# Planner limits, ScalarE squares and DMA moves in a fused attention, mixture-of-experts and MLP kernel

## The chip, the cores and the metric

The kernel runs on 1 core of one Trainium2 chip. The metric is the device time of one execution in microseconds (us), the median of the runs shown.

## The reference

Attention over pooled keys and values gives 4608 tokens of 512 numbers. A router assigns each token to one of 8 experts, in the order of the logits, with 576 places for each expert. Each expert is a two-layer network with a relu, and a shared two-layer network with a squared relu follows.

```python
def _moe_ref(x, w_gate, w1, w2):
    logits = x @ w_gate
    order = np.argsort(-logits.flatten())
    ...
    for idx in order:
        tok, e = int(idx) // E, int(idx) % E
        if assigned[tok] >= 0 or counts[e] >= cap:
            continue
        assigned[tok] = e
        counts[e] += 1
    ...
    for e in range(E):
        mask = assigned == e
        h = np.maximum(x[mask] @ w1[e], 0.0)
        out[mask] = h @ w2[e]

def _moe2_ref(x, w_in, w_out):
    r = np.maximum(x @ w_in, 0.0)
    return (r * r) @ w_out
```

The sizes are: attention 8 batches of 8 heads, 576 positions, 64 wide; experts 512 to 1024 to 512; the shared network 512 to 2048 to 512. All of it is float32.

## The kernel before

The work has three parts. First comes attention, which writes the tokens to DRAM. Then the experts follow one after the other; each expert's 576 tokens run through four products on TensorE (PE). Beside these, from the first expert on, the routing of the later experts runs in the background.

**One expert** is `mlp(n)`, n from 0 to 7. Layer 1 (512 to 1024) and layer 2 (1024 to 512) use the function `layer`, whose matmuls stand at L1249. Layer 3 (512 to 2048) is followed by relu and square, and the last product (2048 to 512, matmuls at L1441 in `last_layer`) is scaled and scattered to the output. A float32 number is carried as two float16 halves, high and low, so each product is three passes (`PASSES`), and each result is split again: ScalarE (ACT) writes the high half, and GpSimd (POOL) or VectorE (DVE) subtracts it to get the low half.

**Layer 3 of expert 0** also goes through `layer` (L1249), with 16 output tiles, each of 576 columns. `plain3` empties a tile: ACT scales it into a float32 work tile (`copy`, L1402), DVE does relu and square in one instruction (`square`, L1411), and `parts1` writes the high half on ACT (L1487) and the low half on POOL (L1488). There are three PSUM buffers for the tiles (`mmt`).

**Layer 3 of experts 1 to 7** needs fewer products, by mixed weights and mixed inputs (seven products instead of eight for each of four output groups, L1386, in the order `ORDER`). It is emptied by `copy` and `relu` on ACT, `join` (L1406) and `square` (L1411) on DVE, and `parts` on ACT and POOL (L1417, L1418). The mixed weights are made by `mix_first` during expert 0 and the start of expert 1: 16 pieces, loaded by SP, combined on POOL, split on ACT and POOL, stored by SP. It sets the event "mixed" when it is done and the loads of the first six have been queued; layer 3 of expert 1 waits for that.

**The background.** The order of all instructions is set while the program is built, by a small planner, the class `Background`. Each engine executes its own instructions in that order. The planner keeps an account in microseconds for PE, ACT, DVE and POOL (`pe`, `a`, `v`, `p`); `work` adds an estimated cost to them. `tick` advances PE's account and goes through the tasks. A task is a generator; it runs on to its next `yield` if the time that it last yielded has come and if the accounts of the engines that it uses are no further ahead of PE's than an allowed depth (2.0 us in most places; for DVE also `vdepth`, 0.9 during layer 3 of experts 1 to 7). A `hold` letter keeps tasks that use that engine from running: the products of layer 3 hold back all that use ACT, except in two places per output group (`slot`). Transfers have no account, except for a fixed delay in the gathers.

The tasks that matter here are these:

- `route(n)` finds the tokens of the expert of number n. It has eight iterations for a threshold, each with two matmul steps on PE (L870 and L884) between DVE steps (L849 is the comparison before L870; L873, L877 and L879 lead to L884). It then makes the indices (`idx`, L999). After a DVE step it yields until DVE's account plus 0.35 us, plus `lazy`, which is 0 for the first two routes and 0.8 for the others. Its uses are "rv"; "r" is a mark with no account.
- `fetch(n)` loads the weights of expert n (SP), finds their scale (L1073) and splits them (L1086 on ACT, L1087 on DVE).
- `gather(n)` fetches the tokens with five indirect transfers on POOL (L1150), converts five pieces (L1188 on ACT, L1189 on DVE, into the tile `gfm`, which has two buffers), and transposes each by a DMA from SP (L1190). For n = 1 a piece is due 12 us (`FLIGHT`) after its gather in POOL's account.
- `split_fixed` splits the shared network's second weight into halves, in place, in eight pieces. Four of them come after layer 2 of expert 0: ACT writes the high half into a `gfm` buffer (L760), DVE the low half into another (L762), and DVE copies both into the place of the weight (L763, L764). The last product of expert 0 waits for all eight.

`wait_next` holds the next expert until its weights and tokens have been planned. `last_layer` of one expert therefore runs beside `fetch` and `gather` of the next.

Of the kernel before, what the change touches and what calls it, by code (L numbers as in the profile page):

```python
# [27 lines left out]
NM = CAP // 128  # L28
# [29 lines left out]
class Background:  # L58
# [6 lines left out]
    def __init__(self):  # L65
        self.pe = self.a = self.v = self.p = 0.0
        self.tasks = []
        self.depth = DEPTH
        self.vdepth = 9.9

    def add(self, gen, uses="av"):
        self.tasks.append([0.0, gen, uses, uses])
# [12 lines left out]
    def tick(self, pe=0.0, hold=""):  # L85

        self.pe += pe
        for t in list(self.tasks):
            while (t[0] <= self.pe and not any(e in t[3] for e in hold)
                   and all(getattr(self, e) <= self.pe + (min(self.depth, self.vdepth) if e == "v" else self.depth)  # L90
                           for e in t[3] if e != "r")):
                try:
                    y = next(t[1]) or 0.0
                except StopIteration:
                    self.tasks.remove(t)
                    break
                t[0], t[3] = y if isinstance(y, tuple) else (y, t[2])
# [8 lines left out]
def moe_kernel(  # L106
# [150 lines left out]
    def later():  # L257
        return bg.pe + 0.1
# [492 lines left out]
    def split_fixed():  # L751
# [3 lines left out]
        for c in range(8):  # L755
            f = words(1, c)
            t = wo[:, c].rearrange("p a b f -> p a (b f)")
            if ("l2", 0) in done:
                hi = r_p.tile([128, 512], F32, name="gfm").bitcast(F16)
                A.activation(hi, f, AF.Copy, scale=K["sout"])  # L760
                lo = r_p.tile([128, 512], F32, name="gfm").bitcast(F16)
                V.scalar_tensor_tensor(lo, f, K["sout"], hi, op0=OP.mult, op1=OP.subtract)  # L762
                V.tensor_copy(t[:, 0], hi)  # L763
                V.tensor_copy(t[:, 1], lo)  # L764
                bg.work(a=1.0, v=1.8)
                yield bg.pe + PACE
                continue
            fs = []
# [29 lines left out]
    def route(n):  # L798

        last = n == E - 1  # L800
        lazy = 0.0 if n < 2 else 0.8
        m, mx = m0, first0
        if n:
            m = r_p.tile([128, NI], F32, name="rm")
# [326 lines left out]
    def gather(n):  # L1131
# [24 lines left out]
        if n == 0:  # L1156
# [14 lines left out]
                bg.work(pe=0.45, a=0.6, v=0.7)  # L1171
                yield 0
            return
        if n == 1:
            while ("l3", 0) not in done:
                yield later()
        for _ in range(NM + 1):
            get()
        if n > 1:
            while ("l3", n - 1) not in done:  # L1180
                yield later()
            at = [max(at[c], bg.pe + 4.0 * c) for c in range(NM + 1)]
        xt[n] = r_p.tile([128, 2, HP, CAP], F16, name="xy", bufs=1)
        for c in range(NM + 1):
            yield at[c]
# [89 lines left out]
    def mlp(n, arrive=None):  # L1275
# [121 lines left out]
        def relu(q, p):  # L1397
            A.activation(q, p, AF.Relu, scale=sg["r"])  # L1398
            bg.work(a=0.7)

        def copy(q, p):
            A.activation(q, p, AF.Copy, scale=sg["r"])  # L1402
            bg.work(a=0.7)

        def join(q, p):
            V.scalar_tensor_tensor(q, p, sg["r"], q, op0=OP.mult, op1=OP.add)  # L1406
            bg.work(v=0.75)

        def square(q):

            V.scalar_tensor_tensor(q, q, 0.0, q, op0=OP.max, op1=OP.mult)  # L1411
            bg.work(v=0.8)

        def parts(q, m, half):

# [54 lines left out]
        if n == 0:  # L1470
# [3 lines left out]
            def plain3(m, p):  # L1474
                if m == 0:
                    first3.append(p)
                    return
                for mz, pz in ([(0, first3[0])] if m == 1 else []) + [(m, p)]:
                    q = qs[3 + mz % 3]
                    copy(q, pz)  # L1480
                    square(q)
                    if mz:
                        parts1(mz - 1)

# [15 lines left out]

        wait("mixed")
        b, a, e = mm(), mm(), mm()
        bg.vdepth = 0.9
        tile[0] = a, b, e
        for j, (gr, i) in enumerate(ORDER):
            if i == 1 and gr:
# [54 lines left out]
                square(c12[gr])  # L1561
                parts(c21[gr], 2 * gr + 8, 0)
            bg.tick(hold="a")
        bg.vdepth = 9.9
        parts(c12[3], 6, 1)
        done.add(("l3", n))
        for _ in last:
# [129 lines left out]
```

## Time and profile before

| | us |
|---|---|
| median of 3 runs | 1422.22 |
| lowest and highest | 1414.69 and 1423.02 |
| the profiled execution | 1418.14 |
| its span in the profile | 1416.4 |

The span runs from the first to the last instruction; 1.7 us lie around it. In the profile PE's matmuls and weight loads (PEld) are shown apart. Where an idle time has a releaser, it is the instruction whose end let the waiting one begin. Stages of the profiled execution were set by their matmuls: expert 0 has layer 3 from 286.4 us and its last product from 348.6 to 404.3 us; layer 3 of experts 1, 2 and 3 begins at 454.3, 606.0 and 756.1 us, and that of expert 6 at 1183.4 us; the last product of expert 2 begins at 651.1 us, layer 1 of expert 3 at 702.2 us, the last product of expert 6 at 1221.9 us. Odd experts have a fifth piece in their last product, which takes the places left over from two experts.

### The profile page before, as it was taken

What the parts mean: (1) busy time and instruction counts of PE and PEld (TensorE: products, weight loads), DVE (VectorE), ACT (ScalarE), POOL (GpSimd) and SP (SyncE); (2) the same over time, 40 slices, a digit from 0 to 9 for tenths busy, and PEclk for the clock granted to TensorE, in tenths of its full rate; (3) what the DMA queues carried; (4) which work ended last, traced back from release to release, by engine and by line L of the source; (5) the groups of instructions that cost most, each with busy time, mean ns of one, the idle gap of its engine ahead of it and who ended that gap; (6) DMA issues with size and microseconds to landing.
All of it is one profiled execution on the core that took longest, in us unless ns stands there. A gap on an engine that the chain in (4) does not pass through costs nothing.

```text
span 1416.4 us, 25407 instructions
## 1 busy us (share of the span) xinstructions
PE 1294.5 (91%) x9925; PEld 918.6 (65%) x9925; DVE 910.2 (64%) x2203; ACT 639.1 (45%) x1241; POOL 450.5 (32%) x449
## 2 busy tenths in 40 slices
PE   6999927887799999998999999999999999999997
PEld 5988826765367755775477646774776477657753
DVE  7889896899577857688767867763354225432620
ACT  5767656543533434243524353354444624462520
POOL 4553041456452441233202320153034203410430
PEclk9989957999899999999999999999999999999999
DMA  9878457213632634142802271047223703470410
GB/s 370 343 298 312 151 193 232 56 31 103 173 99 81 182 98 138 35 121 89 227 5 82 83 227 41 31 135 204 71 84 109 232 8 90 113 204 1 148 33 22
DMA packets 130425, 186.09 MB, mean 131 GB/s; under 512 B 57984, under 2 KB 80512, under 8 KB 125568
## 3 DMA queue, kind: packets, MB, share of 16 engines
q1 hardware_dynamic: 119296, 156.15, 35.4%
q0 software_dynamic: 5824, 18.88, 4.2%
q10 hardware_dynamic: 5184, 9.44, 1.8%
q8 instruction: 77, 1.26, 0.4%
q14 instruction: 44, 0.36, 0.1%
HBM read 143.67 MB, written 30.41 MB: 123 GB/s over the span
## 4 chain that ended last, share of the span: by engine, by line
PE 57%; DVE 19%; issue 4%; ACT 4%; DMA 1%; POOL 1%; SPq 0%; POOLq 0%; ACTq 0%; DVEq 0%
PE mm L1249 21%; PE mm L1441 19%; PE mm L1386 15%; DVE gep L849 2%; DVE qa L1411 2%; DVE e L1087 1%; DMA xy<-gfm 1%; DVE qa L1406 1%; DVE rf L845 1%; DVE hs L1284 1%; DVE rcd L879 1%; DVE wi L1411 1%; DMA hs<-in_w_dram 0%; DVE rpa L889 0%; DVE wo L656 0%
## 5 line engine op out<-in xcount | busy, mean ns | idle before, releaser
L1441 PE MATMUL mm<-wo,g 128*128 128x512 f16 x1728 | 384.6, 381 | 0.0
L1249 PEld LDWEIGHTS <-e 128*128 128x128 f16 x3024 | 292.5, 98 | 79.9 <-issue 6.0
L1441 PEld LDWEIGHTS <-g 128*128 128x128 f16 x1728 | 167.0, 98 | 201.6 <-issue 11.6
L1386 PEld LDWEIGHTS <-wi 128*128 128x128 f16 x2352 | 230.3, 99 | 76.5 <-issue 15.4
L1249 PE MATMUL mm<-hs,e 128*128 128x288 f16 x1536 | 193.4, 286 | 0.0
L1249 PE MATMUL mm<-xy,e 128*128 128x288 f16 x1488 | 188.4, 287 | 1.1 <-DVE hs L1284 1.0
L1386 PE MATMUL mm<-wi 128*128 128x288 f16 x1344 | 179.5, 289 | 8.2 <-DVE wi L1406 7.1
L1386 PE MATMUL mm<-xy,wi 128*128 128x288 f16 x1008 | 135.8, 288 | 4.7 <-DVE qa L1406 3.2
L1418 POOL TENSOR_TENSOR g<-qa,g 128x576 f16<-128x576 f32 x70 | 98.4, 1415 | 110.8 <-ACT g L1417 110.8
L1452 POOL DMA_INDIRECT out_dram<-qa,idx x32 | 33.7, 1053 | 204.0 <-ACT qa L1449 184.2
L1283 ACT ACTIVATE hs<-mm 128x576 f16<-128x576 f32 x64 | 41.5, 650 | 123.7 <-PE mm L1249 110.2
L1087 DVE SCALAR_TENSOR_TENSOR e<-hs,e_s,e 128x1024 f16<-128x1024 f32 (+1 forms) x64 | 76.7, 1246 | 29.3 <-ACT e L1086 29.0
L1402 ACT ACTIVATE qa<-mm,sg_s 128x576 f32<-128x576 f32 x72 | 53.0, 737 | 90.0 <-PE mm L1386 29.9
L1073 ACT ACTIVATE e<-hs 128x1024 bf16<-128x1024 f32 x60 | 63.2, 1053 | 61.5 <-DMA hs<-in_w_dram 60.3
L1284 DVE SCALAR_TENSOR_TENSOR hs<-mm,hs 128x576 f16<-128x576 f32 x64 | 48.0, 755 | 55.6 <-ACT hs L1283 55.4
L1411 DVE SCALAR_TENSOR_TENSOR qa<-qa 128x576 f32<-128x576 f32 x86 | 73.5, 857 | 12.7 <-ACT qa L1398 9.6
L1086 ACT ACTIVATE e<-hs,e_s 128x1024 f16<-128x1024 f32 (+1 forms) x64 | 66.0, 1085 | 32.3 <-DVE e_n L225 26.0
L453 ACT ACTIVATE es<-sc,mb 128x72 f32<-128x72 f32 x288 | 64.4, 340 | 35.1 <-DVE mb L451 35.1
L1406 DVE SCALAR_TENSOR_TENSOR qa<-mm,sg_s,qa 128x576 f32<-128x576 f32 x56 | 45.5, 813 | 50.3 <-ACT qa L1402 45.4
L1418 POOL TENSOR_TENSOR g<-wi,g 128x576 f16<-128x576 f32 x42 | 57.0, 1358 | 57.4 <-ACT g L1417 57.4
L475 PE MATMUL po<-vg,et 72*128 72x73 f32 (+1 forms) x608 | 63.4, 266 | 4.0 <-DVE x L501 3.8
L1417 ACT ACTIVATE g<-qa 128x576 f16<-128x576 f32 x70 | 46.6, 675 | 44.5 <-DVE qa L1411 44.5
(360 smaller groups left out, 1823.7 us busy)
## 6 DMA issues: line engine op xcount, KB each, us to landing
wi<-mixed_weights SPq DMA_DIRECT2D x196, 256.0 KB, 2.7
hs<-in_w_dram SPq DMA_DIRECT2D x60, 512.0 KB, 5.8
tokens_dram<-x ACTq DMA_DIRECT2D x36, 256.0 KB, 5.2
kt<-in_k_dram SPq DMA_DIRECT2D x7, 1152.0 KB, 10.5
vt<-in_v_dram SPq DMA_DIRECT2D x7, 1152.0 KB, 12.2
qt<-in_q_dram SPq DMA_DIRECT2D x7, 1152.0 KB, 8.1
e<-in_win_dram SPq DMA_DIRECT2D x6, 1024.0 KB, 10.1
e<-in_wout_dram SPq DMA_DIRECT2D x4, 1024.0 KB, 5.1
```

Source lines behind the costliest of these rows:

```text
L453: A.activation(es[i][:, x, :], sc[i, x // 4][:, x % 4, :], AF.Exp, scale=1.0 / 64.0, bias=mb[:, x:x + 1])
L475: T.matmul(p[h // 4][o:o + n, (h % 4) * 73:(h % 4) * 73 + 73], lhsT=et[i][:, h, o:o + n], rhs=vg[b][:, h, :], start=True, stop=True)
L1073: A.activation(dst[:, 0, s2, :].bitcast(BF), staged(st, j)[:, s2, :], AF.Square, accum_out=rm[:, c:c + 1])
L1086: A.activation(dst[:, 0], src, AF.Copy, scale=s)
L1087: V.scalar_tensor_tensor(dst[:, 1], src, s, dst[:, 0], op0=OP.mult, op1=OP.subtract)
L1249: T.matmul(p[:, z, 0:HT], lhsT=lh, rhs=mov(b, c)[:, HALVES[z]], start=c == 0 and a + b == 0, stop=c == kk - 1 and a == 1)
L1284: V.scalar_tensor_tensor(halved(h[:, 1, m]), p, 0.0, halved(h[:, 0, m]), op0=OP.max, op1=OP.subtract)
L1386: T.matmul(p[:, z, 0:HT], lhsT=w[:, k, u, z], rhs=yq[:, k, v], start=i in (1, 2, 5) and k == 0 and u + v == 0, stop=k == 1 and u == 1, ski ...
L1406: V.scalar_tensor_tensor(q, p, sg["r"], q, op0=OP.mult, op1=OP.add)
L1411: V.scalar_tensor_tensor(q, q, 0.0, q, op0=OP.max, op1=OP.mult)
L1418: P.tensor_tensor(out=g[:, 1, m:m + 2, gz], in0=q, in1=g[:, 0, m:m + 2, gz], op=OP.subtract)
L1441: T.matmul(o2[c], lhsT=g[:, b, kk, cs], rhs=wo[:, kk // 2, a, kk % 2, :], start=z == 0 and a + b == 0, stop=z == 15 and a == 1)
```

## The change

Seven places change:

- `Background` gets a second depth for DVE, `rdepth`, for tasks with the mark "r" (the routes). In layer 3 of experts 1 to 7 it is 0.4, and `vdepth` for the others goes from 0.9 to 1.6. Outside it is 9.9, so that the general depth of 2.0 holds.
- `lazy` becomes 0 for routes 0 and 1, 0.5 for route 2 and 1.6 from route 3 on (0, 0, 0.8, 0.8 before).
- `join` is accounted at 0.8 us (0.75 before), `square` at 1.1 (0.8 before).
- In `plain3` of expert 0, ACT applies relu with the scale, and a second ACT instruction squares the work tile in place; DVE's `square` is no longer called there.
- In the four late pieces of `split_fixed`, the two DVE copies become two DMAs from SP, and the accounts go from 1.0 to 1.1 for ACT and from 1.8 to 1.4 for DVE.
- `gather(1)` adds `max(at[c], bg.pe + 4.0 * c)` as later experts have it, and 3.0 us on top.
- `gather(n)` for n from 2 on waits for "mixed" before its gathers.

```diff
@@ -66,7 +66,7 @@
         self.pe = self.a = self.v = self.p = 0.0
         self.tasks = []
         self.depth = DEPTH
-        self.vdepth = 9.9
+        self.vdepth = self.rdepth = 9.9
 
     def add(self, gen, uses="av"):
         self.tasks.append([0.0, gen, uses, uses])
@@ -86,9 +86,9 @@
 
         self.pe += pe
         for t in list(self.tasks):
+            room = dict(a=self.depth, p=self.depth, v=min(self.depth, self.rdepth if "r" in t[2] else self.vdepth))
             while (t[0] <= self.pe and not any(e in t[3] for e in hold)
-                   and all(getattr(self, e) <= self.pe + (min(self.depth, self.vdepth) if e == "v" else self.depth)
-                           for e in t[3] if e != "r")):
+                   and all(getattr(self, e) <= self.pe + room[e] for e in t[3] if e != "r")):
                 try:
                     y = next(t[1]) or 0.0
                 except StopIteration:
@@ -760,9 +760,9 @@
                 A.activation(hi, f, AF.Copy, scale=K["sout"])
                 lo = r_p.tile([128, 512], F32, name="gfm").bitcast(F16)
                 V.scalar_tensor_tensor(lo, f, K["sout"], hi, op0=OP.mult, op1=OP.subtract)
-                V.tensor_copy(t[:, 0], hi)
-                V.tensor_copy(t[:, 1], lo)
-                bg.work(a=1.0, v=1.8)
+                nc.sync.dma_start(out=t[:, 0], in_=hi)
+                nc.sync.dma_start(out=t[:, 1], in_=lo)
+                bg.work(a=1.1, v=1.4)
                 yield bg.pe + PACE
                 continue
             fs = []
@@ -798,7 +798,7 @@
     def route(n):
 
         last = n == E - 1
-        lazy = 0.0 if n < 2 else 0.8
+        lazy = (0.0, 0.0, 0.5)[n] if n < 3 else 1.6
         m, mx = m0, first0
         if n:
             m = r_p.tile([128, NI], F32, name="rm")
@@ -1171,15 +1171,13 @@
                 bg.work(pe=0.45, a=0.6, v=0.7)
                 yield 0
             return
-        if n == 1:
-            while ("l3", 0) not in done:
-                yield later()
+        while (("l3", 0) if n == 1 else "mixed") not in done:
+            yield later()
         for _ in range(NM + 1):
             get()
-        if n > 1:
-            while ("l3", n - 1) not in done:
-                yield later()
-            at = [max(at[c], bg.pe + 4.0 * c) for c in range(NM + 1)]
+        while ("l3", n - 1) not in done:
+            yield later()
+        at = [max(at[c], bg.pe + 4.0 * c) + (3.0 if n == 1 else 0.0) for c in range(NM + 1)]
         xt[n] = r_p.tile([128, 2, HP, CAP], F16, name="xy", bufs=1)
         for c in range(NM + 1):
             yield at[c]
@@ -1404,12 +1402,12 @@
 
         def join(q, p):
             V.scalar_tensor_tensor(q, p, sg["r"], q, op0=OP.mult, op1=OP.add)
-            bg.work(v=0.75)
+            bg.work(v=0.8)
 
         def square(q):
 
             V.scalar_tensor_tensor(q, q, 0.0, q, op0=OP.max, op1=OP.mult)
-            bg.work(v=0.8)
+            bg.work(v=1.1)
 
         def parts(q, m, half):
 
@@ -1477,8 +1475,9 @@
                     return
                 for mz, pz in ([(0, first3[0])] if m == 1 else []) + [(m, p)]:
                     q = qs[3 + mz % 3]
-                    copy(q, pz)
-                    square(q)
+                    relu(q, pz)
+                    A.activation(q, q, AF.Square)
+                    bg.work(a=0.7)
                     if mz:
                         parts1(mz - 1)
 
@@ -1500,7 +1499,7 @@
 
         wait("mixed")
         b, a, e = mm(), mm(), mm()
-        bg.vdepth = 0.9
+        bg.vdepth, bg.rdepth = 1.6, 0.4
         tile[0] = a, b, e
         for j, (gr, i) in enumerate(ORDER):
             if i == 1 and gr:
@@ -1561,7 +1560,7 @@
                 square(c12[gr])
                 parts(c21[gr], 2 * gr + 8, 0)
             bg.tick(hold="a")
-        bg.vdepth = 9.9
+        bg.vdepth = bg.rdepth = 9.9
         parts(c12[3], 6, 1)
         done.add(("l3", n))
         for _ in last:
```

## Rows read from the trace of the kernel before

**Rows 1.** The page's busy times, one engine's share of the span.
```profile
PE 1294.5 (91%) x9925; PEld 918.6 (65%) x9925; DVE 910.2 (64%) x2203; ACT 639.1 (45%) x1241; POOL 450.5 (32%) x449
```

**Rows 2.** Windows by stage: stretch, length, busy per engine, granted clock, DMA.
```profile
286.40:348.60 62.20, 49.94 (x427) 38.32 (x425) 57.03 (x136) 25.96 (x38) 39.92 (x40) 1.00 0.16 45
...
348.60:404.30 55.70, 46.45 (x224) 20.35 (x222) 37.80 (x85) 26.25 (x39) 28.43 (x34) 0.91 0.64 176
...
454.30:497.70 43.40, 39.35 (x333) 30.98 (x331) 38.44 (x75) 20.88 (x33) 16.81 (x13) 1.00 0.59 179
...
606.00:651.10 45.10, 41.27 (x334) 31.89 (x333) 38.64 (x82) 21.74 (x33) 17.10 (x14) 0.96 0.43 129
...
651.10:702.20 51.10, 46.48 (x258) 21.91 (x256) 38.05 (x107) 22.68 (x34) 15.05 (x18) 1.00 0.55 152
...
702.20:731.60 29.40, 26.06 (x217) 20.26 (x218) 21.33 (x60) 9.45 (x18) 0.57 (x1) 0.94 0.22 68
...
756.10:804.40 48.30, 42.93 (x339) 32.73 (x338) 40.22 (x87) 21.40 (x33) 18.76 (x15) 0.93 0.39 120
...
1183.40:1221.90 38.50, 38.43 (x315) 30.57 (x313) 24.46 (x42) 21.32 (x33) 18.81 (x15) 1.00 0.54 151
...
1221.90:1266.40 44.50, 44.50 (x221) 21.22 (x220) 13.78 (x19) 21.88 (x33) 8.53 (x12) 1.00 0.61 155
```

**Rows 3.** Waits of PE, 286 to 348.6 us: total, times, longest.
```profile
PE rp L884 <- DVE rcd L879: 6.3, 5, 2.5
...
PE rp L870 <- DVE gep L849: 3.6, 2, 3.1
```

**Rows 4.** DVE by line, late first expert: min/median/max ns, first and last start.
```profile
L1411 DVE SCALAR_TENSOR_TENSOR qa<-qa x16: 745/751/1617, 298.0 to 353.4; 128x576 f32<-128x576 f32 x16
...
L763 DVE COPY wo<-gfm x4: 427/495/1265, 290.8 to 310.7; 128x1024 f16<-128x1024 f16 x4
...
L764 DVE COPY wo<-gfm x4: 419/548/1493, 291.1 to 311.2; 128x1024 f16<-128x1024 f16 x4
...
L762 DVE SCALAR_TENSOR_TENSOR gfm<-wo,wout_s,gfm x4: 1284/1674/1926, 289.3 to 308.8; 128x1024 f16<-128x1024 f32 x4
...
L879 DVE TENSOR_TENSOR rcd<-sel,rcn x7: 283/683/1068, 287.3 to 340.9; 120x120 f16<-120x120 f16 x7
```

**Rows 5.** ACT groups of lines, 286.4 to 360 us: busy, mean ns, idle before.
```profile
L1402 ACT ACTIVATE qa<-mm,sg_s 128x576 f32<-128x576 f32 x16 | 11.7, 736 | 23.7 <-PE mm L1249 21.2 <-DVE sg_s L205 2.5
...
L1487 ACT ACTIVATE g<-qa 128x576 f16<-128x576 f32 x16 | 10.8, 675 | 13.8 <-DVE qa L1411 13.8
...
L760 ACT ACTIVATE gfm<-wo,wout_s 128x1024 f16<-128x1024 f32 x4 | 4.6, 1139 | 2.9 <-DVE wo L763 2.9
```

**Rows 6.** Timeline of PE in the last product: start, length, idle before.
```profile
387.83 0.26 PE L884 MATMUL rp<-rcd,onesh 120*128 120x120 f16 x1 [7.29 <-DVE rcd L879]
...
387.88 6.03 PE L1441 MATMUL mm<-wo,g 128*128 128x512 f16 x18
...
400.44 4.05 PE L1441 MATMUL mm<-wo,g 128*128 128x512 f16 x18
```

**Rows 7.** Timeline of ACT in the same stretch.
```profile
380.83 0.72 ACT L1188 ACTIVATE gfm<-wi,x_s 128x512 f16<-128x512 f32 x1 [5.58 <-DMA xy<-gfm]
```

**Rows 8.** DMA issues, 284 to 410 us: count, KB each, us to landing.
```profile
mixed_weights<-mixb SPq DMA_DIRECT2D x10, 256.0 KB, 2.4
...
xy<-gfm SPq DMA_TRANSPOSE x5, 3.1
```

**Rows 9.** Timeline of SP: a DMA issue after the mixing.
```profile
304.71 0.36 SPq L740 DMA_DIRECT2D mixed_weights<-mixb  x1
```

**Rows 10.** Waits of PE, 404.3 to 930 us.
```profile
PE rp L884 <- DVE rcd L879: 8.3, 5, 3.3
...
PE rp L870 <- DVE gep L849: 4.1, 4, 1.9
```

**Rows 11.** Timeline of DVE: route 3 writes its expert number.
```profile
566.61 0.15 DVE L917 TENSOR_SCALAR ei<-rmw 128x1 int32<-128x1 f32 x1
```

## Prediction

> **What bounds the kernel now.** The page's busy times come first: PE is busy 91% of the span, DVE 64% [rows 1]. So time can only be won where PE stands still. The windows by stage, read next, show where that is [rows 2]. In the last two experts nothing stands still: layer 3 of expert 6 takes 38.5 us with DVE busy 24.46 us, its last product 44.5 us. The same stages of earlier experts are longer. Layer 3 of expert 0 takes 62.2 us with PE busy 49.94 us, so 12.3 us idle, and DVE is busy 57.03 of the 62.2. Expert 0's last product takes 55.7 us with PE busy 46.45 (9.3 us idle). Layer 3 of experts 1, 2 and 3 takes 43.4, 45.1 and 48.3 us, together 21.3 us over three times 38.5. In these stretches the routing of later experts runs on DVE, and its small matmuls sit in PE's queue among the large ones. The waits of PE name them: in layer 3 of expert 0, 6.3 us at L884 and 3.6 us at L870, both for a DVE result of the route [rows 3]. DVE is the bound there through a queue: a route matmul, placed early in PE's order, holds everything behind it until DVE has worked off what stands before its operand.
>
> The profiled execution took 1418.1 us (span 1416.4). The sum below goes against that; it lies inside the three timed runs (1414.7 to 1423.0, median 1422.2). About 1%, 14 us, is what a measurement of this kernel can tell from no change.
>
> **A. Squares of expert 0 on ScalarE, moves by DMA (layer 3 of expert 0).** 16 squares go from DVE; one has a median of 0.751 us and the worst 1.617 [rows 4]: 16 x 0.75 = 12 us and a little more. Of the four late pieces, two copies each go: 4 x (0.495 + 0.548) = 4.2 us by medians. DVE falls from 57 to about 41 us in this stretch. On ACT each tile has cost 0.736 (scaling) + 0.675 (high half) [rows 5]; the new square has no row, so it is bounded by an ACT pass over the same 576 columns from 0.675 to 0.736; I take 0.7. ACT then works 16 x (0.736 + 0.675 + 0.7) = 33.8 us, plus 4.6 for L760, in a stretch of some 50 us: 38 of 50, still beside PE. DVE also drops out of the chain between scaling and high half, where ACT stood 13.8 us [rows 5].
>
> What is late next: the route's own steps. L879 took 0.683 us by median against 0.283 at the shortest [rows 4], while GpSimd works beside it, and that stays. Of the 12.3 us idle I leave 4 and take **8 us** as gained (bounds: 2, if the route packs closer into the freed DVE and waits the same; 12.3, if all goes).
>
> The eight DMAs stand on SP. Each pair waits there for L762's result (1.9 us at worst, rows 4), and behind it stand the loads and stores of the mixing. An issue takes 0.36 us [rows 9], so 8 x 0.36 = 2.9 us of SP, and a copy of the same 256 KB landed in 2.4 us [rows 8]. The copies that they replace ended at about 312 us [rows 4], the weights are first read by the last product from 348.6 us: 36 us of cover, **0 us** on the path. Without that cover a last pair would cost about 1.9 + 2.4 + 0.7 = 5 us.
>
> **B. The last product of expert 0.** The longest single wait is here: 7.29 us at L884, then 18 matmuls in 6.03 us at a lower granted clock where 18 later ones took 4.05 [rows 6], 2 us more. The cause stands on ACT: the third token conversion waited 5.58 us for the transposing DMA that still read its buffer (there are two) [rows 7]; DVE's half of the conversion and then the route's L879 were queued behind it. The title says the conversions are paced. Worked out, they are not: the five gathers push the due times to T+13 to T+17 in steps of 1, the 4c term reaches at most T+16, and so the new line only adds 3 us to each: T+16 to T+20. The two buffers still fill, and conversions 3 to 5 still wait one landing each, 3.1 us by median [rows 8], instead of 5.6 for the first. What the shift buys is distance from the expert's weight loads. The wait should drop to about 3 or 4 us, short of the fall of the clock: 7.3 + 2 - 3.5 = **6 us** gained (bounds: -3, by which the tokens come later with nothing else late; 9.3). The new guard on the mixing, for expert 2 and later, costs 0: layer 3 of expert 1 waits for the same event from 454.3 us on, and route 2, which those gathers need, is then still on its way. The tokens themselves have cover, as nothing at the start of the next layer 1 waits for them.
>
> **C. Layer 3 of experts 1 to 3.** The planner now lets a route piece out only when its DVE account is at most 0.4 us ahead (0.9 before), counts a square as 1.1 and a join as 0.8, and a route from number 3 on waits 1.6 instead of 0.8 us after each DVE step before its matmul is queued. Per output group the account had 3 x 0.75 + 4 x 0.8 = 5.45 us, now 3 x 0.8 + 4 x 1.1 = 6.8, so fewer route pieces fit. The DVE surplus of these stages over expert 6 is 14 to 16 us each [rows 2]. I take half of the 21.3 us: **10.5 us** (bounds: 3 and 18). It is an estimate: nothing in the trace shows a route at the new spacing.
>
> **D. Last products and layers 1 of experts 2 and 3.** Layer 1 of expert 3 has 29.4 - 26.06 = 3.3 us idle, the last product of expert 2 51.1 - 46.48 = 4.6 [rows 2]. The extra 0.8 us of lead per step gives DVE time to catch up; against it stand the pieces moved out of layer 3. **4.5 us** gained (bounds -5 and 8).
>
> **E. What the delay moves back.** Routes 5 to 7, done by about 900 us before, reach into experts 4 and 5, which were clean: **4 us** lost (0 to 12). Route 3 wrote its expert number at 566.6 us [rows 11], 39 us ahead of the layer 3 at 606 us in which its weights are fetched; 8 steps of twice 0.8 us are 13 us, so nothing is late there. Route 2 gets less spacing (0.5), in its favour.
>
> Sum: 1418.1 - 8 - 6 - 10.5 - 4.5 + 4 = 1393, so **1393 us**. By all good ends it would be about 1371 (12.3 + 9.3 + 18 + 8 = 47.6), by all bad ends about 1433 (2 - 3 + 3 - 5 - 12 = -15).
>
> **Rivals.** *The waits only move (1410).* The gain of A and B comes (14 us), but what layer 3 gives up the route takes back in the last products and layers 1 and in experts 4 and 5: 1418 - 14 + 6 = 1410. For it: the total work of the routes is unchanged. Against: the clean experts have DVE room (24 of 38.5 us busy).
>
> *Held-back route pieces pay more where they land (slower).* Place: the last products and layers 1 of experts 1 to 4, where weight halves and conversions stand in DVE's queue. If about 9 iterations leave layer 3 (3 each) and each pays two matmul waits of 2 us, that is 36 us against 25 us from A, B and C: 1418 + 11 = 1429. It decides from 25 / 9 = 2.8 us per iteration. Against: between 404 and 930 us, L884 and L870 lost 8.3 + 4.1 us [rows 10] in some 40 iterations, 0.3 us each; for: single ones reached 3.3.
>
> *ScalarE becomes the bound in layer 3 of expert 0 (1406).* If a square took 2.25 us (three of DVE's 0.75), ACT would need 16 x (0.736 + 0.675 + 2.25) = 58.6 us plus 4.6 for L760 and a few of mixing, about 67 against the 62.2 us before: 5 us lost where 8 were to be won, 1393 + 13 = 1406. Against: ACT passes of this size run at 0.7 us, shorter than DVE's. The Trainium skill (ScalarE: Activation LUTs, section Rules for kernel authors) speaks for this rival: simple functions and multiplications belong on VectorE, which it puts at up to about three times faster for bf16 with one source. The trace disagrees for this fp32 tile: 0.751 us on DVE, 0.675 on ACT [rows 4, 5].
>
> **How the numbers follow.** The forecast has a chance of 0.62 (its own range 1374 to 1408); the waits only move 0.22; pieces pay more 0.10; ScalarE bound 0.06. The range 1374 to 1422 takes in the second and fourth whole and leaves about 0.16 outside, most of it above. Faster by over 1%, below 1408: 0.59 of the forecast, 0.05 and 0.02 of the second and fourth, 0.66. Within 1%: 0.03 + 0.17 + 0.04 = 0.24. Slower: 0.10.
>
> **What would show it.** A: layer 3 of expert 0 near 54 us, no L1411 there, DVE near 41 us. B: the longest wait at L884 in the last product under 4 us, no stretch of low clock after it; the spacing of the conversions still set by the landings. C: 40 to 44 us for layer 3 of experts 1 to 3. E: route 7 later than 900 us, and small waits in experts 4 and 5. The forecast is wrong if PE's waits at L870 and L884 after 404 us grow instead of shrink, or if layer 3 of expert 0 stays above 58 us with ACT the releaser.

## The result and the profile after

The changed kernel took 1407.27 us (median of 20 runs, 1398.0 to 1425.66), the kernel before 1420.51 us (20 runs): ratio 0.9907, 95% interval 0.9882 to 0.9932. That is 13 us or 0.9% less. 25 us had been forecast from the profiled execution, 29 us from the median of the runs before it (1422.2 to 1393). So the direction was right and the time lies inside the stated range, but the gain is only about half of the forecast. The profiled execution took 1415.4 us, longer than the median. The reason stands ahead of the changed stages: expert 0 began at 244.1 us in it, where it began at 229.5 us in the profile before, and no instruction up to there differs. From the start of layer 3 of expert 0 to the end it is 1413.6 - 301.5 = 1112.1 us against 1416.4 - 286.4 = 1130.0, 17.9 us less. So the stages are compared from there on.

Windows by stage of the changed kernel: stretch, length, busy time of PE, PEld, DVE, ACT, POOL, granted clock (1.00 is the full one), DMA share, GB/s.

```profile
301.50:357.80 56.30, 50.88 (x442) 38.57 (x441) 48.71 (x134) 38.39 (x58) 31.85 (x35) 1.00 0.35 113
357.80:410.40 52.60, 44.98 (x220) 20.12 (x219) 34.56 (x86) 23.92 (x36) 25.66 (x31) 0.94 0.56 144
434.80:465.40 30.60, 24.50 (x216) 19.04 (x214) 22.26 (x72) 9.96 (x18) 11.63 (x16) 1.00 0.18 51
465.40:513.00 47.60, 42.45 (x325) 32.56 (x326) 31.34 (x57) 19.62 (x30) 24.55 (x19) 0.89 0.66 214
617.10:658.70 41.60, 39.18 (x327) 30.88 (x325) 32.05 (x67) 20.86 (x33) 17.65 (x13) 1.00 0.61 190
658.70:703.90 45.20, 45.20 (x239) 21.72 (x237) 30.56 (x72) 26.00 (x39) 9.65 (x12) 1.00 0.56 137
703.90:727.90 24.00, 24.00 (x207) 19.22 (x206) 15.23 (x49) 5.88 (x15) 0.97 (x1) 1.00 0.04 13
752.30:793.70 41.40, 39.15 (x327) 30.88 (x325) 32.06 (x67) 20.85 (x33) 17.64 (x13) 1.00 0.59 191
...
1178.00:1219.20 41.20, 38.59 (x315) 30.48 (x313) 25.26 (x42) 23.33 (x37) 17.46 (x14) 1.00 0.62 192
```

Against [rows 2], in this order: layer 3 of expert 0 went from 62.2 to 56.3 us, with DVE busy 48.7 instead of 57.0 and ACT 38.4 instead of 26.0; its last product from 55.7 to 52.6. The third line is layer 2 of expert 1 with the wait before its layer 3; it has grown by 5.4 us from 25.2. Layer 3 of experts 1, 2 and 3 (lines 4, 5 and 8) takes 47.6, 41.6 and 41.4, where it took 43.4, 45.1 and 48.3. The last product of expert 2 and layer 1 of expert 3 (lines 6 and 7) have no idle time left: 69.2 us where it was 80.5. Layer 3 of expert 6, clean before with 38.5 us, takes 41.2, and its DMA share rose from 0.54 to 0.62. Layer 3 of experts 4 and 5 grew as well, by 1.7 and 3.2 us.

Waits of PE in the changed kernel, 300 to 1420 us: in total, times, longest.

```profile
PE mm L1384 <- DMA wi<-mixed_weights: 21.3, 7, 5.4
PE rp L236 <- DVE rsm L232: 7.0, 1, 7.0
...
PE rp L870 <- DVE gep L849: 1.5, 3, 0.6
PE rp L884 <- DVE rcd L879: 1.1, 2, 0.9
```

The waits for the route at L884 and L870, which led before [rows 3, 6, 10], are down to 1.1 and 1.5 us in the whole stretch, from 21.9 and 7.8 us. In their place PE waits seven times for the mixed weights of layer 3, a transfer that it never waited for before, and once for 7 us in the last product of expert 0.

Where the waits for mixed weights come from is read in SP's order. Timeline of SP in layer 3 of expert 5, then the same stretch of PE, then the DMA issues (KB each, median us from issue to landing) from 1034 to 1056.4 us and from 1056.4 to 1066 us:

```profile
1035.68 19.96 SPq L1271 DMA_DIRECT2D wi<-mixed_weights  x14
1056.46 2.28 SPq L1063 DMA_DIRECT2D hs<-in_w_dram  x4
1058.85 11.48 SPq L1271 DMA_DIRECT2D wi<-mixed_weights  x8
```

```profile
1066.86 1.64 PE L1384 MATMUL mm<-wi 128*128 128x288 f16 x12 [2.76 <-DMA wi<-mixed_weights]
```

```profile
wi<-mixed_weights SPq DMA_DIRECT2D x14, 256.0 KB, 2.6
...
hs<-in_w_dram SPq DMA_DIRECT2D x4, 512.0 KB, 6.2
wi<-mixed_weights SPq DMA_DIRECT2D x6, 256.0 KB, 7.4
```

Four loads of 512 KB, the next expert's first weights, now stand in the middle of the stream of 256 KB loads that feeds layer 3. Before, SP issued nothing but mixed weights in this layer and the loads came behind it. A mixed weight issued ahead of them landed after 2.6 us (median), one issued behind them after 7.4. The first one behind them was issued at 1058.85 us and landed 8.0 us later, and there, at 1066.86 us, the wait of PE ended. SP's own delay is the smaller part: its stream paused for 3.5 us between two mixed weights, where the usual step is 1.5 us. The same four loads stand inside layer 3 of experts 1 to 6 in the changed kernel; in the kernel before only in that of expert 1, and there behind its last mixed weight.

The two profiles of the changed kernel (the second is the first experiment) say how far a single one can be read: a stage differs between them by up to 2.4 us, layer 3 of expert 0 by less than 0.1 us.

### The profile page after: what moved, and what is told of

Read it like the earlier page. It is cut to its first block, busy times and chain, and to the rows that moved or that the text cites. A ratio compares the mean times of both kernels' runs of the same rounds, so it can differ in the third digit from the quotient of the medians.

```text
span 1413.6 us, 25395 instructions
## 1 busy us (share of the span) xinstructions
PE 1305.9 (92%) x9925; PEld 932.5 (66%) x9925; DVE 886.7 (63%) x2179; ACT 645.6 (46%) x1257; POOL 440.8 (31%) x449
## 4 chain that ended last, share of the span: by engine, by line
PE 62%; DVE 10%; DMA 5%; issue 4%; ACT 3%; POOL 2%; SPq 0%; POOLq 0%; ACTq 0%; DVEq 0%
PE mm L1247 22%; PE mm L1439 22%; PE mm L1384 16%; DMA wi<-mixed_weights 4%; DVE gep L849 2%; DVE wo L656 1%; DVE hs L1282 1%; DVE rf L845 1%; DVE xy L1322 0%; ACT qa L1309 0%; DMA xy<-gfm 0%; ACT xy L1320 0%; DVE e L1087 0%; PE rp L870 0%; POOL wi L1335 0%
## 5 line engine op out<-in xcount | busy, mean ns | idle before, releaser
L1384 PEld LDWEIGHTS <-wi 128*128 128x128 f16 x2352 | 229.6, 98 | 87.2 <-DMA wi<-mixed_weights 23.5
L1384 PE MATMUL mm<-wi 128*128 128x288 f16 x1344 | 177.4, 287 | 15.9 <-DMA wi<-mixed_weights 15.9
L1384 PE MATMUL mm<-xy,wi 128*128 128x288 f16 x1008 | 135.8, 289 | 6.7 <-DMA wi<-mixed_weights 5.4
L1281 ACT ACTIVATE hs<-mm 128x576 f16<-128x576 f32 x64 | 41.6, 650 | 131.5 <-PE mm L1247 114.6
L1087 DVE SCALAR_TENSOR_TENSOR e<-hs,e_s,e 128x1024 f16<-128x1024 f32 (+1 forms) x64 | 75.1, 1217 | 24.3 <-ACT e L1086 24.0
L1447 ACT ACTIVATE qa<-mm,uo 128x512 f32<-128x512 f32 x32 | 22.0, 686 | 123.9 <-PE mm L1439 98.5
L1409 DVE SCALAR_TENSOR_TENSOR qa<-qa 128x576 f32<-128x576 f32 x70 | 66.6, 951 | 15.8 <-ACT qa L1396 13.9
L1073 ACT ACTIVATE e<-hs 128x1024 bf16<-128x1024 f32 x60 | 62.7, 1046 | 28.3 <-DMA hs<-in_w_dram 27.3
L475 PE MATMUL po<-vg,et 72*128 72x73 f32 (+1 forms) x608 | 73.2, 288 | 1.9 <-DVE x L501 1.7
L1086 ACT ACTIVATE e<-hs,e_s 128x1024 f16<-128x1024 f32 (+1 forms) x64 | 66.1, 1084 | 18.1 <-DVE e_s L223 13.9
L475 PEld LDWEIGHTS po<-vg,et 72*128 72x128 f32 (+1 forms) x608 | 71.4, 205 | 4.0 <-DVE x L501 2.9
```

The costliest lines, as they stand in the source:

```text
L475: T.matmul(p[h // 4][o:o + n, (h % 4) * 73:(h % 4) * 73 + 73], lhsT=et[i][:, h, o:o + n], rhs=vg[b][:, h, :], start=True, stop=True)
L1073: A.activation(dst[:, 0, s2, :].bitcast(BF), staged(st, j)[:, s2, :], AF.Square, accum_out=rm[:, c:c + 1])
L1086: A.activation(dst[:, 0], src, AF.Copy, scale=s)
L1087: V.scalar_tensor_tensor(dst[:, 1], src, s, dst[:, 0], op0=OP.mult, op1=OP.subtract)
L1384: T.matmul(p[:, z, 0:HT], lhsT=w[:, k, u, z], rhs=yq[:, k, v], start=i in (1, 2, 5) and k == 0 and u + v == 0, stop=k == 1 and u == 1, ski ...
```

## The experiments

All were timed in five rounds beside the kernel before. A ratio is the recorded one to it, with its 95% interval; it can differ from the quotient of the two medians (at most by 0.3%: 0.9808 where that is 0.9836). The first four runs, the next four (squares, copies with their old account, route limits, mixing) and the last four were timed on three chips, so between these groups only ratios and stages are compared. Stages come from one profile each. Each diff is against the changed kernel.

**The changed kernel again** (no edit).

> The changed kernel once more, as a control. In its first profile the first expert began at 244.1 us, in that of the kernel before at 229.5, though not one instruction before that point differs. Theory chance: the attention part varies from execution to execution; here the first expert begins somewhere between 229 and 245 us, and the ratio to before is again 0.985 to 0.995. Rival: the later begin belongs to the change; then it begins near 244 us again and the kernel before near 230. Waits of PE for mixed weights: about 21 us in sum again if the order of the loads causes them; under 5 us if that one execution had slow transfers.

Ratio 0.9893 (0.9852 to 0.9933). Expert 0 began at 230.7 us, and the waits for mixed weights were 20.9 us in seven places. So the late begin in the first profile is chance, and the waits are not. From layer 3 of expert 0 on it took 1404.2 - 288.1 = 1116.1 us, 13.9 less than before.

**The limit for the other DVE tasks at 0.9.**

```diff
-        bg.vdepth, bg.rdepth = 1.6, 0.4
+        bg.vdepth, bg.rdepth = 0.9, 0.4
```

> The changed kernel with the depth for other DVE tasks in layer 3 back at 0.9 (the routes stay at 0.4). Theory (weight loads admitted into layer 3 delay the mixed weights): the loads of the next expert's weights move behind layer 3 again, PE's waits for mixed weights fall from 21 us to about 5 (the one at the start of layer 3 of expert 1, which hangs on the mixing, stays), layer 3 of experts 4 to 6 takes 38.5 us again instead of 41 to 41.7; 10 to 15 us faster than the changed kernel, ratio to before about 0.980 to 0.985. Rival (slow transfers in that execution): nothing moves, ratio 0.99. Against the gain: weight halves come later, and the 5 us in layer 1 of expert 3 may return.

Ratio 0.9864 (0.9827 to 0.9902). Timeline of SP in layer 3 of expert 5, then waits of PE from 225 us on:

```profile
1024.00 31.48 SPq L1271 DMA_DIRECT2D wi<-mixed_weights  x22
1071.03 1.29 SPq L1188 DMA_TRANSPOSE xy<-gfm  x1
1073.64 0.96 SPq L1063 DMA_DIRECT2D hs<-in_w_dram  x2
```

```profile
PE rp L236 <- DVE rsm L232: 12.7, 5, 7.2
...
PE mm L1384 <- DMA wi<-mixed_weights: 5.3, 1, 5.3
```

The mechanism is as expected: the loads are behind the layer, the waits fall from 21 to 5.3 us, layer 3 of experts 5 and 6 takes 38.5 us. The gain is not: the interval overlaps that of the changed kernel. What comes later is waited for later. The last product of expert 4 and layer 1 of expert 5 take 50.2 and 28.1 us, together 8.8 more than in the changed kernel, and the waits at L236, for the scale of the weights, are 12.7 us where they were 8.1 us from 225 us on. So the limit of 1.6 both gave (early weights) and took (late mixed weights), and nearly evenly.

**The conversions of expert 1 really spaced.**

```diff
-        at = [max(at[c], bg.pe + 4.0 * c) + (3.0 if n == 1 else 0.0) for c in range(NM + 1)]
+        at = [(at[0] + 4.0 * c) if n == 1 else max(at[c], bg.pe + 4.0 * c) for c in range(NM + 1)]
```

> The changed kernel with the conversions of expert 1 really 4 us apart (due at the first one's time plus 4 us each) instead of 1 us apart and 3 us later. Theory (two buffers, each held until its transposing DMA has landed, block ACT and DVE): the 7.0 us wait at L236 and the low clock after it go, the last product of expert 0 takes 44 to 47 us instead of 52.7, 6 to 8 us in all, if the mixing does not take it back before layer 3 of expert 1. Rival (the tokens come too late, or the mixing is the next bound): the last product gets shorter, but a wait of the same size stands at layer 1 or layer 3 of expert 1, no gain in sum.

Ratio 0.9798 (0.9759 to 0.9838), against 0.9893 on the same chip. The last product of expert 0, its window:

```profile
353.58:398.13 44.55, 42.60 (x221) 19.37 (x219) 32.95 (x80) 23.93 (x34) 25.77 (x29) 1.00 0.61 154
```

44.6 us instead of 53.3 (the changed kernel again, same chip), with the full clock. The wait at L236 is gone. This was the largest gain that a single edit to the changed kernel brought in a stage, 8.7 us, and no new wait came in its place at the start of expert 1, where the rival had one.

**Both edits.** The two diffs above together.

> Both edits. If the two theories hold and are independent, 16 to 22 us faster than the changed kernel, ratio to before about 0.975 to 0.98. If the mixing bounds the start of layer 3 of expert 1, only the first of the two counts.

Ratio 0.9764 (0.9728 to 0.9801). As expected, the two gains nearly add up: 17 us by medians against the changed kernel on the same chip. The profile had one wait for mixed weights left, 4.9 us, at the start of layer 3 of expert 1.

**The squares of expert 0 back on VectorE.**

```diff
-                    relu(q, pz)
-                    A.activation(q, q, AF.Square)
-                    bg.work(a=0.7)
+                    copy(q, pz)
+                    square(q)
```

> The changed kernel with expert 0's squares on VectorE again (scale on ScalarE, relu and square on DVE at L1411), all else changed. Theory (the squares are what DVE was short of in layer 3 of expert 0): that layer takes 60 to 62 us again instead of 56.2, PE's waits for the route there 9 to 12 us instead of about 5, ratio to before 0.993 to 0.996 where the changed kernel has 0.990. Rival (the moves by DMA and the lighter planner account are the cause): layer 3 of expert 0 stays at 56 to 58 us, ratio as that of the changed kernel.

Ratio 0.9937 (0.9910 to 0.9964), as the theory had it, but not in the place that it had named. Layer 3 of expert 0 took 57.3 us, as the rival had it, only 1.1 more than with the squares on ACT. Layer 1 of expert 1 took 30.8 us instead of 24.3, with a wait of 3.8 us at L884 and a clock of 0.89. DVE work that is not done in one stage is waited for in the next, so the price of a stage's edit isn't read in that stage alone. One stage got shorter: layer 2 of expert 1 took 24.4 us instead of 30.6, without a wait for mixed weights at its end. The mixing ended 13 us earlier than in the changed kernel (lines below, under the mixing), so with the squares ScalarE also took on a delay of the mixing.

**The four pairs of copies back on DVE**, with their old account.

```diff
-                nc.sync.dma_start(out=t[:, 0], in_=hi)
-                nc.sync.dma_start(out=t[:, 1], in_=lo)
-                bg.work(a=1.1, v=1.4)
+                V.tensor_copy(t[:, 0], hi)
+                V.tensor_copy(t[:, 1], lo)
+                bg.work(a=1.0, v=1.8)
```

> The changed kernel with the four late pairs of copies on DVE again. Theory (4 to 6 us of DVE work, half of it behind other work): layer 3 of expert 0 gets 1 to 3 us longer than 56.2, ratio 0.990 to 0.992. Rival: the DMAs were what mattered in that layer, 60 us or more.

Ratio 0.9831 (0.9807 to 0.9855): faster than the changed kernel, which neither theory had. The last product of expert 0 fell to 50.6 us and the layer before it to 53.9. Two more runs took the edit apart.

**Copies on DVE, with the account of the changed kernel**, so that the order on every engine stays but for the moves; and **the moves by DMA, with the old account**.

```diff
-                nc.sync.dma_start(out=t[:, 0], in_=hi)
-                nc.sync.dma_start(out=t[:, 1], in_=lo)
+                V.tensor_copy(t[:, 0], hi)
+                V.tensor_copy(t[:, 1], lo)
```

```diff
-                bg.work(a=1.1, v=1.4)
+                bg.work(a=1.0, v=1.8)
```

> The changed kernel with the four pairs of copies on DVE, but the planner's account for them left at 1.1 and 1.4, so that every engine's order is that of the changed kernel but for the moves themselves. The kernel with the copies and the old account was at 0.983. Theory (order: the account shifts the routes against the conversions of expert 1, the moves themselves are worth 0 to 3 us in favour of the DMA): the last product of expert 0 keeps its 7 us wait at L236 and takes 52 to 54 us, ratio 0.989 to 0.993. Rival (the DMAs themselves cost, through SP's queue): last product near 50 us, ratio 0.983.

> The other half: moves by DMA as in the changed kernel, the account back at 1.0 and 1.8. Theory (order): as the kernel with copies and old account, last product of expert 0 near 50.6 us, ratio 0.981 to 0.985. Rival (the DMAs cost): last product 52 to 54 us, ratio near 0.989.

Ratios 0.9919 (0.9886 to 0.9951) and 0.9808 (0.9768 to 0.9849). Waits of PE in the last product of expert 0, first of the former, then of the latter:

```profile
PE rp L236 <- DVE rsm L232: 7.1, 1, 7.1
```

```profile
PE rp L884 <- DVE rcd L879: 3.4, 1, 3.4
```

It is the account. With the new numbers the scale of the weights stands behind the conversions, whoever moves the data; with the old ones a route step stands there and loses half as much. What the moves themselves are worth hangs on that order. With the new account layer 3 of expert 0 took 60.3 us with copies and 56.2 with DMAs, 4 us in favour of the DMA; with the old one it took 53.9 with copies and 55.3 with DMAs, 1.4 us the other way.

**Route 2's lead at 0.8 again.**

```diff
-        lazy = (0.0, 0.0, 0.5)[n] if n < 3 else 1.6
+        lazy = (0.0, 0.0, 0.8)[n] if n < 3 else 1.6
```

> The changed kernel with route 2's lead at 0.8 us again instead of 0.5; nothing else. Theory (what stands behind the conversions of expert 1 in the last product of expert 0 is a matter of where route 2's and the weight scale's steps fall, and any shift moves it): the last product of expert 0 changes by 2 us or more from 53 us; if the lead is what made it 47.0 in the kernel with the old route limits, it falls to 47 to 49 us and the ratio to 0.984 to 0.987. Rival (the collision hangs on the conversions alone): 52 to 54 us, ratio 0.989.

Ratio 0.9807 (0.9768 to 0.9846). The wait at L236 was 3.3 us, the stage 47.3 us. The time is 14 us below that of the changed kernel, but from the beginning of expert 0 on the profile has 1168.4 us against 1169.6 and 1173.5 in the changed kernel's two: 1 to 5 us. Where the rest of the difference in time lies isn't shown. This is a third edit, beside the spacing and the account, that shortens the same wait; the changed kernel sits at a bad place among them.

**The route limits as before.**

```diff
-        lazy = (0.0, 0.0, 0.5)[n] if n < 3 else 1.6
+        lazy = 0.0 if n < 2 else 0.8
...
-            bg.work(v=0.8)
+            bg.work(v=0.75)
...
-            bg.work(v=1.1)
+            bg.work(v=0.8)
...
-        bg.vdepth, bg.rdepth = 1.6, 0.4
+        bg.vdepth, bg.rdepth = 0.9, 0.9
```

> The changed kernel with the planner's route limits as before (0.9 for all, extra lead 0.8, accounts 0.75 and 0.8); ScalarE squares, DMA moves and the 3 us shift of expert 1's conversions stay. Theory (holding the routes back pays in layer 3 of experts 2 and 3, in the last product of expert 2 and layer 1 of expert 3, about 25 us, and the limit of 1.6 gives back some 10 us in experts 4 to 6): layer 3 of experts 2 and 3 near 45 and 48 us again, layer 3 of experts 4 to 6 near 38.5 to 39.3, no waits for mixed weights but the one at the start of layer 3 of expert 1; ratio 0.995 to 1.000. Rival (the whole gain comes from expert 0): ratio 0.985 to 0.990.

Ratio 0.9905 (0.9883 to 0.9927), between the two expectations: the kernel is as fast as the changed one. By stage, four of its windows (layer 3 of expert 2, the last product of expert 2, layer 1 of expert 3, layer 3 of expert 6):

```profile
593.40:637.40 44.00, 39.77 (x334) 31.20 (x333) 38.41 (x82) 21.51 (x33) 17.13 (x14) 1.00 0.46 133
637.40:689.60 52.20, 46.31 (x258) 22.02 (x255) 37.85 (x109) 22.83 (x34) 15.00 (x18) 1.00 0.63 164
689.60:719.10 29.50, 26.14 (x217) 20.36 (x217) 20.98 (x58) 9.45 (x18) 0.00 (x0) 0.94 0.11 41
...
1169.80:1208.30 38.50, 38.43 (x315) 30.57 (x314) 24.38 (x42) 21.34 (x33) 18.82 (x15) 1.00 0.53 151
```

The losses of experts 2 and 3 are back, as the theory had it: the middle two lines are together 12.5 us longer than in the changed kernel. The clean layer 3 of expert 6 is back too. What it had missed: the last product of expert 0 takes 47.0 us here instead of 52.6, with route 2's old lead, which by itself gave 47.3. So this run takes out the holding back and puts in that gain. Its fair partner is the changed kernel with only the lead at 0.8 (the run above): 0.9807 against 0.9905 here, intervals apart, and 1168.4 against 1174.4 us from the beginning of expert 0 on. The route limits, the 1.6 included, are thus worth 6 us in the profiles and more in the times; against the changed kernel this doesn't show, since that one has the worse lead.

**Quicker mixing**, on top of the limit of 0.9 and the spaced conversions.

```diff
             bg.work(p=2.1)
-            yield bg.p + 2.0
+            yield bg.p + 0.5
```

> The kernel with depth 0.9 and spaced conversions, and the mixing's planned pause per piece cut from 2.0 to 0.5 us, so that its 16 pieces end earlier. Theory (the mixing now bounds the start of layer 3 of expert 1): the wait of 4.9 us for mixed weights there goes, layer 2 of expert 1 takes 24 to 26 us instead of 29.6; 4 to 5 us faster than the kernel with the two edits, ratio 0.972 to 0.974. Rival (denser mixing on POOL, ACT and SP costs as much in layer 3 of expert 0 and in the last product): no gain, 0.976.

Ratio 0.9741 (0.9709 to 0.9774). As the theory had it, layer 2 of expert 1 takes 24.6 us instead of 29.6 and no wait for mixed weights is left. The 5 us stand in the stage; as a time they are within the intervals of 0.9764 and 0.9741.

**All of these**, with the copies on DVE and their old account.

> Depth 0.9, spaced conversions, quicker mixing, and the copies on DVE with their old account. The same without the last was at 0.974. Theory (the order theory: with spaced conversions the collision is gone, so the copies' shift has nothing to win): 0.973 to 0.977. Rival (the DMAs cost by themselves): 0.965 to 0.970.

Ratio 0.9750 (0.9703 to 0.9797). As the theory had it: once the conversions are spaced, the copies' shift of the order has nothing left to win. Either of the last two kernels is about 2.5% faster than the kernel before and 1.6% faster than the changed one.

## Why the prediction was wrong in size

**The steps that failed.** The forecast's sum followed DVE's time and the route's matmuls, and put the transfers of layer 3's mixed weights at nothing, in two places: the mixing, of which it says only that the new guard on it "costs 0", and C and E, which give no price to the limit of 1.6 for the other DVE tasks. The runs showed 21.3 us of PE waits for mixed weights: 5.4 us for the end of the mixing and 15.9 us behind early weight loads. The third is B, "the wait should drop to about 3 or 4 us": it stayed at 6.99 us, and the stage won 3.1 us instead of 6. The terms one by one:

**A (8 us for layer 3 of expert 0): 5.9 us in the stage, the mechanism only in part shown.** The new square measured as it was taken, 0.683 us against 0.7. ACT was busy 38.4 us where 38 had been worked out; that it fits so well is luck, since the sum left out L1073 and the mixing's L736 (3.1 and 1.8 us in this layer) and counted tiles that fall behind it. ACT groups of lines of the changed kernel, 301 to 360 us:

```profile
L1396 ACT ACTIVATE qa<-mm,sg_s 128x576 f32<-128x576 f32 x16 | 11.7, 733 | 10.9 <-PE mm L1247 10.8
L1479 ACT ACTIVATE qa<-qa 128x576 f32<-128x576 f32 x16 | 10.9, 683 | 0.5
```

ACT waits for PE and no longer for DVE, so ScalarE did not become the bound, and that rival falls. The DVE forecast of 41 us was too low (48.7): the route packed closer into the freed time, which had been named as the lower bound; its instructions took 43.0 us of DVE in this layer, 31.5 before. With the squares back on DVE the layer lost only 1.1 us, and with the copies back in the same order 4; the squares paid mostly in layer 1 of expert 1 (6.5 us), which the sum did not have, and nearly as much was lost again in layer 2, through the mixing. The eight DMAs cost nothing on the path, as said; that their planner account would shift the order had not been said.

**B (6 us for the last product of expert 0): failed.** The reading that the pacing is only a shift was right, and so was the cause that it named, two buffers held until their transposing DMAs land (spacing the conversions took the wait away). But the step "the wait should drop to about 3 or 4 us, short of the fall of the clock" was not. Timeline of ACT, then of DVE, then of PE, in the changed kernel:

```profile
389.54 0.72 ACT L1186 ACTIVATE gfm<-wi,x_s 128x512 f16<-128x512 f32 x1 [2.31 <-DMA xy<-gfm]
...
394.40 0.72 ACT L1186 ACTIVATE gfm<-wi,x_s 64x512 f16<-64x512 f32 x1 [3.24 <-DMA xy<-gfm]
```

```profile
395.15 0.74 DVE L1187 SCALAR_TENSOR_TENSOR gfm<-wi,x_s,gfm 64x512 f16<-64x512 f32 x1 [3.21 <-ACT gfm L1186]
...
398.52 0.15 DVE L232 TENSOR_REDUCE rsm<-rmx 128x1 bf16<-128x4 f32 x1
```

```profile
369.17 6.64 PE L1439 MATMUL mm<-wo,g 128*128 128x512 f16 x30
...
398.73 0.18 PE L236 MATMUL rp<-rsm,onesb 128*128 128x1 bf16 x1 [6.99 <-DVE rsm L232]
...
398.99 8.97 PE L1439 MATMUL mm<-wo,g 128*128 128x512 f16 x30
```

The longest wait of ACT for a landing did get shorter, 3.2 us (another took 2.3) instead of 5.6 [rows 7], but behind the last conversion on DVE now stood the end of a route step and then the scale of the weights, and PE waited 6.99 us where it had waited 7.29 [rows 6]. 30 matmuls behind it took 8.97 us at a granted clock of 0.74, where 30 others took 6.64 us in the same product: the clock had fallen as before. Nor was a wait of 3 or 4 us "short of the fall of the clock": in the run with the old route limits PE waited 3.29 us in this product, and the 30 matmuls behind it took 7.91 us (granted clock 0.74 from 378 to 383 us). PE stood 7.6 us in the whole stage instead of 9.3 and was busy 1.5 us less; these are the 3 us that it did win. Route 2's smaller lead, which the prediction counted as "in its favour", worked against it here: with 0.8 us the wait is 3.3 us and the stage 47.3 us.

**The guard and the mixing ("costs 0"): half right.** The guard itself cost nothing. But the mixing behind it had not been followed: counted from the start of expert 0, PE reaches layer 3 of expert 1 8.9 us earlier, and the mixing ends 5.9 us later (441.4 - 229.5 = 211.9 us before, 461.9 - 244.1 = 217.8 after). The stores of the mixed pieces in the kernel before, the changed one, and the changed one with the squares on DVE (its expert 0 began at 234.5 us):

```profile
L740 SPq DMA_DIRECT2D mixed_weights<-mixb x16: 359/360/382, 260.6 to 441.4; - x16
```

```profile
L740 SPq DMA_DIRECT2D mixed_weights<-mixb x16: 359/359/537, 275.8 to 461.9; - x16
```

```profile
L740 SPq DMA_DIRECT2D mixed_weights<-mixb x16: 359/360/618, 267.5 to 439.2; - x16
```

With the squares on DVE the mixing ends after 439.2 - 234.5 = 204.7 us. So with all else as changed, the squares on ScalarE, which also splits the mixed pieces, make it 13 us later; whether through ACT's time or through the planner's account for it was not tried apart. The other edits bear on it too: with the old route limits it ends after 210.5 us. SP, POOL and PE in the changed kernel at this point:

```profile
448.44 13.79 SPq L740 DMA_DIRECT2D mixed_weights<-mixb  x2
462.27 16.99 SPq L1271 DMA_DIRECT2D wi<-mixed_weights  x14
```

```profile
460.48 1.37 POOL L737 TENSOR_TENSOR mixb<-mixb 128x512 f16<-128x512 f32 x1
```

```profile
465.39 4.65 PE L1384 MATMUL mm<-xy,wi 128*128 128x288 f16 x24 [5.42 <-DMA wi<-mixed_weights]
```

SP stands at the store of the last mixed piece until POOL has made it; the loads for layer 3 are queued behind, and PE waits 5.42 us. The quicker mixing showed it by taking this away.

**C (10.5 us for layer 3 of experts 1 to 3): 6.3 us in the stages.** Experts 2 and 3 won 3.5 and 6.9, expert 1 lost 4.2: inside its layer PE waited 5.2 us for mixed weights behind the early loads, and it was busy 3.1 us longer at a granted clock of 0.89 instead of 1.00. With the limit at 0.9 this layer took 40.6 us. **D (4.5 us): 11.3 us**, but about half of it comes from the early weight loads: with the routes held and the limit at 0.9 these two stages take 75.0 us, with the limit at 1.6 they take 69.2, with the old limits 81.7.

**E (4 us back): 7.6 us in layer 3 of experts 4 to 6, from another cause.** Routes were expected there. They did come later (route 7 wrote its expert number at 1015.0 us, 900.2 before), but PE's waits in these layers were for mixed weights. What failed is that the limit of 1.6 for the other DVE tasks, which stands in the same line as the 0.4, was priced nowhere. It lets the next expert's `fetch` into the layer, and a fetch begins with 2 MB of loads on SP. The steps of C counted DVE's account and no DMA.

In sum -5.9 - 3.1 - 6.3 - 11.3 + 7.6, the 5.4 of the mixing and -4.3 in the other stages (what is left over) give the 17.9 us of the profile. C, D and E come to -10.0 us, near the forecast of -11, but by luck: D gave 6.8 us more than forecast, and C and E together missed by 7.8 us. The second profile has 13.9 us and the medians 13, so part of what is missing is the difference between executions.

Of the rivals, "the waits only move" came nearest in time (1410 against 1407), but not in kind. It had all 14 us of A and B come, and 9.0 came; it had the routes take back what layer 3 gives up, in the last products and layers 1, and these won 11.3 us. What was taken back went to a transfer. From "held-back pieces pay more" nothing was seen. The sign that was named for being wrong, growing waits at L870 and L884, did not show: these waits shrank, and the new ones stand at L1384 and L236, where the prediction did not look.

## What to carry to other kernels

When a planner's limit is raised for a class of tasks, list everything that such a task issues, its DMAs first, and the queue that it will now stand in. A planner without an account for transfers can move a wait from an engine to a queue without seeing it. And after any change of accounts or leads, look at the one or two places where a chain of buffer, transfer and conversion blocks an engine: shifts there were worth 9 to 14 us by the ratios (the copies' account, route 2's lead), and with the chain spaced out the one of them that was tried, the copies' account, changed nothing.

## What had not been expected of the hardware

The part before the experts, the same instructions in every kernel here, ended between 227.3 and 244.1 us in the fourteen profiles. Its windows, of the changed kernel's two executions:

```profile
0.00:244.10 244.10, 189.31 (x1814) 177.88 (x1815) 196.34 (x546) 147.92 (x440) 88.86 (x83) 0.79 0.68 256
```

```profile
0.00:230.70 230.70, 174.16 (x1814) 162.88 (x1815) 195.75 (x546) 147.36 (x440) 88.97 (x83) 0.85 0.72 271
```

DVE, ACT and POOL were busy for the same time in both; PE was busy 15 us longer, with the same instructions at a lower granted clock (0.79 against 0.85). That one stretch is as large as the whole effect of the change, so two single executions could have shown it with either sign. Why the clock is lower in some executions was not tried and stays open.
